# Spectral filter and gated feed-forward, forward and backward: all row-tile transposes in the head, the transform of x as pieces of the loop

## The chip, the core and the metric

The kernel runs on one core of a Trainium2 chip. The metric is the device time of one execution in microseconds (us). TensorE is called PE, its weight loads PEld, VectorE DVE, ScalarE ACT, GpSimd POOL, and SyncE, which issues most DMAs, SP.

## What is computed

The reference is the forward result of a gated mix and the gradients of its inputs:

```python
g = sigmoid((x * gate_w).sum(-1, keepdims=True))       # one gate per row
a = irfft2(rfft2(x) * (w_r + 1j * w_i))                # spectral filter over both axes
b = (gelu(x @ w_gate) * (x @ w_up)) @ w_down           # feed-forward
out = g * a + (1 - g) * b                              # then the gradients by vjp with grad_out
```

x and grad_out (dO below) are 2048 x 576, w_gate and w_up 576 x 4608, w_down 4608 x 576, the filter 2048 x 289, all bf16. Outputs are `out`, the gradients of x, w_r, w_i, w_gate, w_up, w_down, gate_w. The two-dimensional transforms are matrix products with tables of sines: along the 576 columns with `Dt`, along the 2048 rows in two stages, first with `Rt` (within what one row tile holds), and, after a pass through DRAM, with the 32-point table `B`. The same is done for x and for dO, then the products with the filter, then the way back (`RT`, `BT` and `Dt` again).

## The kernel before

**Data.** The rows are dealt out as 16 row tiles of 128. `xn` and `dB` hold x and dO with rows on partitions; `xT` and `dOT` hold them turned, with the 576 columns on partitions in five chunks (the last has 64). A turn of four row tiles (`tchunk`, L335) is 16 full transposes and 8 half ones on PE into three PSUM tiles and three copies to SBUF, of 1024, 1024 and 512 elements per partition.

**Three stages.** The *head* loads x and dO, builds the tables on DVE, ACT and POOL (`build_D`, `build_R`, `columns_B`, `build_B`), turns the row tiles, does the whole forward transform of x, and at its end computes the gate (`gate`, L355, 80 matmuls of one column and a sigmoid). The *loop* goes over 18 groups g of 256 feed-forward columns and, in each, over m = 0 to 3, four row tiles at a time: 72 rounds, called passes here, numbered 4 g + m. The *last part* multiplies what the loop put into DRAM (`scr`) by the weights once more, and forms `out` and the gradients of x and gate_w.

**A pass.** `H_mm` (L370) multiplies dOT by w_down into the PSUM tile z (L380, L383), and xT by w_gate and w_up into two PSUM tiles xy (L387, L394). ACT copies z to `da` (L404), and xy to `q` (squared), `xb` and `hu` (L411 to L414). `H_ew1` (three DVE operations, L419 to L421) gives the argument s of the sigmoid; `H_ew2` is two sigmoids on ACT, om and s (L435, L436), and eight DVE operations (L440 to L447) that leave A, dHg and dHu. SP stores them to `scr`. The tiles q and s have one buffer each. From group 1 on a pass also does a part of the weight gradients of the group before, `W_units`: halves of 16 or 8 matmuls (L480, L497, L510) into a PSUM pool of two buffers, with a copy on ACT (L458) and a DMA from POOL at the end of a unit. `scale_dB` (L932) scales dB by 1 - g in two halves after passes 3 and 4.

**Spectral pieces.** The rest of the transforms is cut into pieces, the list `fft`, which `fft_next` calls one after the other. A forward row tile has two: u1 (L546), six matmuls (L551) and a copy Y on ACT (L556, L558), and u2 (L561), two matmuls (L568), a copy ve on ACT (L572), two DVE operations that leave Vt (L574, L575) and a store to `scr_x` or `scr_g` (L576). `zipped` lists them as u1(0), u1(1), u2(0), u1(2), u2(1) and so on. Behind the 32 pieces of dO come the tables turned for the way back (three pieces), 74 slots of the middle (`mid_units`: s2 with two copies of 64 partitions each, L666, s1 with one copy, L753, and seven empty slots ahead; the products with the filter are DVE work, called in portions by `side_work`), and 64 pieces of the inverse. 175 slots in all. In group 0 pieces take turns in two PSUM tiles, pg and z; from group 1 on the feed-forward's z tile is the only one.

**Order.** It is written by hand: each engine's queue has the instructions in the order in which the program calls them, and an engine waits at its first instruction that isn't ready. `want(pr)` says how many pieces are to be done after a pass: 4 per pass in group 0, and then as many as make an even load up to pass 64, where a slot of the middle counts 1.7. That is 3 or 4 per pass in passes 4 to 10, mostly 2 up to pass 47, and 3 or 4 to pass 64. In a pass of group 1 and later the first piece stands inside the second half of xy, and the next ones between the weight halves, when the weights' nominal time `at` reaches 0, 1, 3 and 5; the sigmoids (`sigs`, which calls `H_ew2`) are put in at 1.0:

```python
for w, f in carry + hs:
    if k < n and at >= (0.0, 1.0, 3.0, 5.0)[k]:
        fft_next()
        k += 1
    if late and at >= 1.0:
        late.pop()()
    f()
    at += w
```

In the head, x's pieces use the same four PSUM tiles as the transposes in turn (`headps`, L330), x's first pieces follow the first four row tiles, and the other turns stand between them. gate_w comes as a column by three small DMAs from POOL (L852, L853).

Of the kernel before, what the change touches and what calls it, by code (L numbers as in the profile page):

```python
# [140 lines left out]
def build_R(nc, tb, unit, t0):  # L141

    V = nc.vector
    n = 4
    step = 2.0 * math.pi / S * EPS_SCALE
    X = unit([n, P], I32, name="XR")
    krow, kadd = tb.kk[:, 0, :], tb.kk[:, 1, :]
    for t in range(n):
        V.scalar_tensor_tensor(X[:, t, :], krow, tb.scol[:, t0 + t:t0 + t + 1], kadd, op0=ALU.mult, op1=ALU.add)
    V.tensor_single_scalar(X[:], X[:], S - 1, op=ALU.bitwise_and)  # L150
    if t0 % 8 == 0:
        tb.Rpair = unit([8, P], name="Rt")
    o = tb.Rpair[:, t0 % 8:t0 % 8 + n, :]
    tb.late.append(lambda: nc.scalar.activation(o, X[:], ACT.Sin, bias=tb.pi[:], scale=-step))
    tb.Rt += [tb.Rpair[:, t0 % 8 + t, :] for t in range(n)]
# [36 lines left out]
def build_B(nc, tb, unit, res):  # L192
# [10 lines left out]
    for s in range(2):  # L203
        G.iota(mask[:, 0, :, :, :, s], pattern=[[0, 2], [1 - 2 * s, 2], [0, 16]], base=s, channel_multiplier=0, **kw)
    X = unit([2, 2, 16, 2], F32, name="XB")
    Xi = unit([2, 2, 2, 16, 2], I32, name="XBi")
# [13 lines left out]
    def sines():  # L220
        nc.scalar.activation(o[:], Xi[:].rearrange("p v a b c d -> p v (a b c d)"), ACT.Sin, bias=tb.pi[:], scale=-step)
        V.tensor_tensor(tb.B[:], o[:], ms[:].rearrange("p v a b c d -> p v (a b c d)"), op=ALU.mult)
    tb.late.append(sines)


@with_exitstack
def kernel(
# [31 lines left out]
    xn = res.tile([P, T, D], BF16, name="xn")  # L259
    gwT = res.tile([P, 5], BF16, name="gwT")  # L260
    xT = hres.tile([P, 5, T, P], BF16, name="xT")
    dOT = hres.tile([P, 5, T, P], BF16, name="dOT")
# [5 lines left out]
    def load_w(g, part):  # L268

        fsl = slice(g * FG, (g + 1) * FG)  # L270
        if part == 0:
            wts[g] = (wpool.tile([P, 5, 2 * FG], BF16, tag="wgu", name="wgu"), wpool.tile([P, 5, FG], BF16, tag="wdT", name="wdT"))
            wgu = wts[g][0]
# [16 lines left out]

    nc.gpsimd.memset(gwT[LO, 4:5], 0.0)
    ident = res.tile([P, P], BF16, name="ident")
# [7 lines left out]

    for k in range(4):
        load_x(4 * k)
    for k in range(4):
        load_do(4 * k)
    load_w(0, 0)

    ew = wstack.enter_context(tc.tile_pool(name="ew", bufs=2))
# [26 lines left out]

    def tchunk(src, dst, t0, copy=None):  # L335
        for k, cs in enumerate(((0, 1), (2, 3), (4,))):
            pool, tag = headps()
            tp_ = pool.tile([P, 2, 2, 4, P], BF16, tag=tag, name="tp")
            for j, c in enumerate(cs):
                for tt in range(4):  # L340
                    if c < 4:
                        nc.tensor.transpose(tp_[:, 0, j, tt, :], src[:, t0 + tt, eo(c)], ident[:])
                    else:
                        for r in (LO, HI):
                            nc.tensor.transpose(tp_[r, 0, 0, tt, :], src[:, t0 + tt, 512:D], ident[:])
            o = dst[:, cs[0]:cs[0] + len(cs), t0:t0 + 4, :]
            i = tp_[:, 0, 0:len(cs)]
            if copy:
                copy(o, i)
            elif k == (t0 // 4) % 2:  # L350
                nc.scalar.copy(o, i)
            else:
                V.tensor_copy(o, i)

    def gate():  # L355
        lps = head_tile()[:, 0]
        for t in range(T):
            for ci in range(5):
                nc.tensor.matmul(lps[:, t:t + 1], lhsT=xT[:, ci, t, :], rhs=gwT[:, ci:ci + 1],
                                 start=(ci == 0), stop=(ci == 4))  # L360
        nc.scalar.activation(g_bf[:], lps[:, 0:T], ACT.Sigmoid)
        V.tensor_copy(g32[:], g_bf[:])
        V.tensor_scalar(omg_bf[:], g32[:], -1.0, 1.0, op0=ALU.mult, op1=ALU.add)
        V.tensor_copy(omg32[:], omg_bf[:])
        V.tensor_scalar(gs32[:], g32[:], SD2, None, op0=ALU.mult)
# [176 lines left out]

    def fwd_units(src, dst, scale, ps=pftile, vevac=None):
        ys = {}
# [16 lines left out]
        def u2(t):  # L561
            def f():
                Y = ys.pop(t)
                R = tb.Rt[t]
                vps = ps()
                Yf = Y[:].rearrange("p e c l -> p (e c) l")
                for o, ys_ in enumerate((Yf[:, 0:4:3, :], Yf[:, 2:0:-1, :])):
                    nc.tensor.matmul(vps[:, o, :2 * HF].rearrange("p (e l) -> p e l", e=2), lhsT=R, rhs=ys_, start=True, stop=True)  # L568
                Vt = (unit if src is xT else half)([2, DF], name="Vt")
                ve = unit([2, 2, HF], F32, name="ve")  # L570
                n0 = 1 if src is xT or on_pg() else 0
                nc.scalar.copy(ve[:, n0:2].rearrange("p o c l -> p o (c l)"), vps[:, n0:2, :2 * HF])  # L572
                v = [vps[:, 0, :2 * HF].rearrange("p (c l) -> p c l", c=2) if n0 else ve[:, 0], ve[:, 1]]
                V.tensor_tensor(Vt[:, :, 0:HF], v[0], v[1], op=ALU.add)  # L574
                V.tensor_tensor(Vt[:, :, DF - 1:HF - 1:-1], v[0][:, :, 0:HF - 1], v[1][:, :, 0:HF - 1], op=ALU.subtract)  # L575
                LD.dma_start(dst[:, t], Vt[:])  # L576
# [263 lines left out]

    def head_tile():
        pool, tag = headps()
        return pool.tile([P, 2, 512], F32, tag=tag, name="fx")

    build_D(nc, tb, unit, res, 0, 2)
    build_D(nc, tb, unit, res, 2, 2)
    tchunk(xn, xT, 0, V.tensor_copy)
    build_D(nc, tb, unit, res, 4, 1)
    columns_B(nc, tb, res)
    with nc.allow_non_contiguous_dma(reason="tiny gate_w column load"):  # L850
        for par in range(2):
            nc.gpsimd.dma_start(gwT[:, 2 * par:2 * par + 2], gate_w[par:512:2].rearrange("(k p) -> p k", p=P))  # L852
        nc.gpsimd.dma_start(gwT[HI, 4:5], gate_w[512:D].rearrange("(p o) -> p o", o=1))  # L853
    x1, x2 = fwd_units(xT, scr_x, None, ps=head_tile)
    build_R(nc, tb, unit, 0)
    run_late(tb)
    for t in range(T):
        x1[t]()
        if t in (6, 11):
            load_w(0, 1 + t // 11)  # L860
        if t % 4 == 2 and t < 14:
            tchunk(xn, xT, t + 2)
        if t >= 9 and t % 2 == 1:
            tchunk(dB, dOT, 2 * (t - 9))
        if t % 4 == 1 and t + 3 < T:
            build_R(nc, tb, unit, t + 3)
        if t == 13:
            build_B(nc, tb, unit, res)
        if tb.late:
            tb.late.pop(0)()  # L870
        if t > 1:
            x2[t - 2]()
    run_late(tb)
    x2[T - 2]()
    x2[T - 1]()
    gate()

    fg = zipped(*fwd_units(dOT, scr_g, gs32))
    ia, pa = inv_units(scr_p1, a_dv, SD2)
# [15 lines left out]
    n_slots = sum(1 for u in fft if not getattr(u, "noslot", False))  # L895
    mid_at = 2 * T + 10
    NPR = NT // 2
    LASTP = NG * NPR - 7
    done = [0]

    def want(pr):

        n0 = 4 * NPR
        if pr < NPR:
            return 4 * (pr + 1)

        def load(n):

            return n + 0.7 * min(max(n - mid_at, 0), n_mid)
        share = load(n0) + (load(n_slots) - load(n0)) * (pr + 1 - NPR) / (LASTP - NPR)  # L910
# [24 lines left out]
    for g in range(NG):  # L935
# [3 lines left out]
        for m in range(NPR):  # L939
# [5 lines left out]
            def side_work(us):  # L945
                while side and us > 0:
                    us -= side[0][0]
                    side.pop(0)[1]()
            if g == 0 and m > 0:
                fft_next()  # L950
            z, xy_full = H_mm(g, m)
# [4 lines left out]
            flush()  # L956
            if g == 0:
                fft_next()
            if pr == 0:
                fft_next()  # L960
            H_act(0, xy, tiles, 1)
            state = []

            def second():
                xy = xy_full(1, fft_next if n or g == 0 else None)
                for part in range(2):
                    H_act(1, xy, tiles, part)
                state.append(H_ew1(tiles))
                side_work(1.4)

            def sigs():
                H_ew2(g, m, tiles, state[0], da)
                side_work(1.4)
            if g == 0:
                second()
                fft_next()
                sigs()
            else:
                second()
                at, k, late = 0.0, min(n, 1), [sigs]  # L980
                for w, f in carry + hs:
                    if k < n and at >= (0.0, 1.0, 3.0, 5.0)[k]:
                        fft_next()
                        k += 1
                    if late and at >= 1.0:
                        late.pop()()
# [5 lines left out]
                if late:  # L992
                    sigs()
            carry = []
            flush(len(stores) - 1)
# [251 lines left out]
```

## Time and profile before

| what | us |
| --- | --- |
| median of five runs | 1455.92 |
| the five runs | 1461.59, 1462.19, 1455.92, 1454.86, 1455.90 |
| the profiled execution's own time | 1461.59 |
| its span, first to last instruction | 1459.8 |
| PE busy in the span | 1395.4 (96%) |
| DVE busy | 731.6 (50%) |
| ACT busy | 715.3 (49%) |
| POOL busy | 125.7 (9%) |
| mean granted PE clock | 0.992 |

The profile is of one execution. Its span leaves 1.8 us of its own time outside. It gives for every instruction the engine, the source line, the tiles that it writes and reads, its start and duration, and for idle time what ended it. A row of a stretch gives, after its limits and length, the busy time of PE, PEld, DVE, ACT and POOL in it with the number of instructions, then the granted clock, the share of the DMA engines and GB/s. A row of waits gives the waiting instruction, what it waited for, the sum, the count and the longest. A row in order of time gives start, duration, engine, line, operation, tiles, and in square brackets the idle time before it. A PE row's duration takes in the drain of its last matmul, so the time from start to start is the shorter and is what a dense stream pays.

### The profile page before, as it was taken

Reading aid. Unit: us, or ns where it says so; the run is one execution under the profiler, and the core shown is the slowest. Engines: PE = TensorE matmul, PEld = TensorE weight load, DVE = VectorE, ACT = ScalarE, POOL = GpSimd, SP = SyncE. Lnnn points to the kernel's source line nnn. Section 1 sums busy time; section 2 is a strip of 40 time slices with the busy share of each in tenths; the row PEclk is TensorE's granted clock in tenths of the full one; section 3 lists DMA queues with packets and bytes.
Section 4 is the critical chain, followed back from the end, with each engine's and each line's share of the span. In section 5 each row is a group of like instructions: output and inputs, shape, how many; then the busy total and the mean of one; then the engine's idle time right before and its main releaser. Section 6 shows DMA issues by size and latency. Waiting matters only on the chain.

```text
span 1459.8 us, 28184 instructions
## 1 busy us (share of the span) xinstructions
PE 1395.4 (96%) x11414; PEld 1024.3 (70%) x11414; DVE 731.6 (50%) x1394; ACT 715.3 (49%) x1311; POOL 125.7 (9%) x230
## 2 busy tenths in 40 slices
PE   6888899998999999999999999999999999999997
PEld 4555675675676667667767767668777777777776
DVE  6676556876776676755656556552000652212200
ACT  5776767777677777666766766663000000000000
POOL 3000010010011011001001001100000110000000
PEclk9999999999999999999999999999999999999999
DMA  5333354544644554463554653848999997887773
GB/s 190 94 103 104 100 162 110 146 120 137 164 121 132 143 157 116 114 170 89 154 145 120 161 156 105 193 126 203 214 192 195 217 205 160 168 160 158 163 148 75
DMA packets 516477, 214.96 MB, mean 147 GB/s; under 512 B 312921, under 2 KB 510554, under 8 KB 516346
## 3 DMA queue, kind: packets, MB, share of 16 engines
q1 hardware_dynamic: 506714, 192.65, 56.4%
q0 software_dynamic: 7824, 19.49, 4.5%
q8 instruction: 89, 1.46, 0.4%
q10 hardware_dynamic: 1808, 1.02, 0.2%
q14 instruction: 42, 0.34, 0.1%
HBM read 40.76 MB, written 93.84 MB: 92 GB/s over the span
## 4 chain that ended last, share of the span: by engine, by line
PE 80%; ACT 9%; DVE 4%; DMA 2%; issue 2%; SPq 1%; POOL 0%; ACTq 0%; DVEq 0%; POOLq 0%
PE acc L1092 29%; PE xy L394 15%; PE wps L497 14%; PE z L380 8%; PE wps L480 6%; PE xy L387 2%; PE wps L510 2%; ACT om L435 2%; PE z L383 1%; ACT xb L413 1%; ACT hu L414 1%; ACT q L411 1%; DMA wd_all<-in_B_w_down_dram 1%; ACT Xx L666 1%; DMA out_dram<-dw 1%
## 5 line engine op out<-in xcount | busy, mean ns | idle before, releaser
L1092 PEld LDWEIGHTS <-pin 128*128 128x128 bf16 x3456 | 338.3, 98 | 87.6 <-issue 1.5
L394 PE MATMUL xy<-wgu,xT 128*128 128x512 bf16 x1152 | 272.6, 381 | 0.0
L497 PEld LDWEIGHTS <-xn 128*128 128x128 bf16 x2304 | 224.6, 98 | 38.0 <-issue 0.2
L394 PEld LDWEIGHTS <-xT 128*128 128x128 bf16 x1152 | 106.4, 98 | 137.1 <-issue 30.9
L404 ACT ACTIVATE da<-z,omg 128x256 bf16<-128x256 f32 x288 | 112.8, 474 | 117.8 <-PE z L383 117.8
L480 PE MATMUL wps<-dB,A 128*128 128x288 bf16 x1152 | 152.1, 286 | 12.4 <-ACT dwd L458 12.4
L1109 ACT COPY bo<-acc 128x288 f32<-128x288 f32 x32 | 12.8, 399 | 308.2 <-PE acc L1092 250.1
L380 PE MATMUL z<-wdT,dOT 128*128 128x256 bf16 x1152 | 139.0, 274 | 14.8 <-ACT Y L558 4.2
L1092 PE MATMUL acc<-wgT,pin 128*128 128x288 bf16 x1152 | 145.3, 288 | 0.8 <-ACT dw L458 0.8
L480 PEld LDWEIGHTS <-A 128*128 128x128 bf16 x1152 | 112.1, 98 | 45.7 <-issue 15.0
L1092 PE MATMUL acc<-wuT,pin 128*128 128x288 bf16 x1152 | 143.6, 286 | 0.0
L1092 PE MATMUL acc<-wd_all,pin 128*128 128x288 bf16 x1152 | 142.6, 286 | 0.0
L380 PEld LDWEIGHTS <-dOT 128*128 128x128 bf16 x1152 | 112.2, 98 | 34.6 <-issue 19.9
L497 PE MATMUL wps<-dHg,xn 128*128 128x256 bf16 x1152 | 135.8, 273 | 0.0
L497 PE MATMUL wps<-dHu,xn 128*128 128x256 bf16 x1152 | 133.8, 273 | 0.0
L411 ACT ACTIVATE q<-xy 128x512 bf16<-128x512 f32 x144 | 86.9, 604 | 55.9 <-PE xy L394 54.0
L419 DVE TENSOR_SCALAR s<-q 128x1024 bf16<-128x1024 bf16 x72 | 30.7, 426 | 159.5 <-ACT q L411 159.5
L440 DVE TENSOR_TENSOR xb<-xb,s 128x1024 bf16<-128x1024 bf16 x72 | 49.9, 693 | 108.3 <-ACT s L436 108.3
L503 POOL DMA_DIRECT2D out_dram<-dw x67 | 48.8, 728 | 632.0 <-ACT dw L458 526.9
L1169 DVE SCALAR_TENSOR_TENSOR f32t<-gwf,dlog,b16t 128x576 f32<-128x576 f32 x16 | 13.1, 817 | 173.7 <-DMA b16t<-dxa_scr 173.7
L414 ACT CAST hu<-xy 128x512 bf16<-128x512 f32 x144 | 88.3, 613 | 0.0
L413 ACT CAST xb<-xy 128x512 bf16<-128x512 f32 x144 | 84.8, 589 | 0.0
(197 smaller groups left out, 1594.3 us busy)
## 6 DMA issues: line engine op xcount, KB each, us to landing
scr<-A SPq DMA_DIRECT2D x72, 256.0 KB, 2.6
scr<-dHg SPq DMA_DIRECT2D x72, 256.0 KB, 2.8
scr<-dHu SPq DMA_DIRECT2D x72, 256.0 KB, 3.3
out_dram<-dw POOLq DMA_DIRECT2D x67, 128.0 KB, 2.3
wd_all<-in_B_w_down_dram SPq DMA_DIRECT2D x3, 1728.0 KB, 16.6
out_dram<-dwd POOLq DMA_DIRECT2D x34, 144.0 KB, 2.9
scr_p<-Vt SPq DMA_DIRECT2D x32, 145.0 KB, 3.5
wgu<-in_B_w_gate_dram SPq DMA_DIRECT2D x18, 256.0 KB, 3.7
```

Of the source, the lines that this page charges most:

```text
L380: nc.tensor.matmul(zo(t), lhsT=dOT[:, ci, t, :], rhs=wdT[:, ci, :], start=(t % 4 < 2 and ci == 0), stop=False)
L394: nc.tensor.matmul(xy[k][:, t % 2, :], lhsT=xT[:, ci, t, :], rhs=wgu[:, ci, :], start=False, stop=(ci == 3))
L404: nc.scalar.activation(da[:, t, :], z[:, t % 2, t // 2, :], ACT.Copy, scale=omg32[:, 4 * m + t:4 * m + t + 1])
L411: nc.scalar.activation(q[:, h, :], xy[:, :, 0:FG], ACT.Square)
L413: nc.scalar.copy(xb[:, h, :], xy[:, :, 0:FG])
L414: nc.scalar.copy(hu[:, h, :], xy[:, :, FG:2 * FG])
L419: V.tensor_scalar(s[:], q[:], A_GELU, 1.0, op0=ALU.mult, op1=ALU.add)
L440: V.tensor_tensor(xb[:], xb[:], s[:], op=ALU.mult)
L480: nc.tensor.matmul(wps[:, :288], lhsT=tl(0, t)[:, fch * P:(fch + 1) * P], rhs=dB[:, t, h * 288:(h + 1) * 288], start=(t == 0), stop=(t == ...
L497: nc.tensor.matmul(wps[:, cc, :], lhsT=xn[:, t, (c0 + cc) * P:(c0 + cc + 1) * P], rhs=tl(k, t), start=(t == 0), stop=(t == T - 1))
L503: wst[0].dma_start(ov[:, c0:c0 + TPB, fsl], dw[:])
L1092: nc.tensor.matmul(acc[:, :288], lhsT=src[:, r, :], rhs=w_of(r)[:, h * 288:(h + 1) * 288], start=(first and r == 0), stop=(last and r == F ...
```

## The change

It does six things.

1. The head turns all row tiles of x and dO, in the order x, dO, x, dO, and does nothing of the transform of x. Which engine copies each of the three PSUM tiles of a turn is written out by hand (`VC` is a DVE copy, `AC` an ACT copy).
2. The transform of x becomes the first 32 pieces of `fft`, which now has 207 slots. x's Vt takes the pool `half` of two buffers, as dO's did.
3. Group 0 does 0, 1, 1 and 2 pieces in its four passes (`FIRST` holds the sums). Later passes share the rest evenly up to pass 64, with a slot of the middle counting 1.5: 3 in pass 4, 4 each in passes 5 to 18, 2 or 3 (4 in passes 20 and 21) up to pass 49, and 4 each in passes 50 to 64.
4. In a pass with four or more pieces they stand at 0, 1, 2, 3.6 and 5, and the sigmoids at 1.6. `side_work` takes larger portions.
5. R tables 8 to 15 and the table B are begun in group 0, between passes; their sines on ACT run at the end of pass 4.
6. SP loads x and dO in turns, with the transposing loads of w_down's first group after the first of each. gate_w comes as a row by one DMA from SP, and five matmuls with a 1 x 1 tile of one turn it into the column.

```diff
+    gwr = unit([D], name="gwr")
+    LD.dma_start(gwr[0:1, :], gate_w.rearrange("(o d) -> o d", o=1))
+    load_x(0)
+    load_do(0)
+    load_w(0, 1)
+    for k in range(1, 4):
         load_x(4 * k)
-    for k in range(4):
         load_do(4 * k)
     load_w(0, 0)
+    load_w(0, 2)
...
-                Vt = (unit if src is xT else half)([2, DF], name="Vt")
+                Vt = half([2, DF], name="Vt")
...
+    gps = head_tile()[:, 0]
+    for c in range(5):
+        w = gwr[0:1, eo(c)] if c < 4 else gwr[0:1, 512:D]
+        r = slice(0, P) if c < 4 else HI
+        nc.tensor.matmul(gps[r, c:c + 1], lhsT=w, rhs=one[:], start=True, stop=True)
+    AC(gwT[:, 0:4], gps[:, 0:4])
+    AC(gwT[HI, 4:5], gps[HI, 4:5])
     build_D(nc, tb, unit, res, 0, 2)
+    turn(xn, xT, 0, (VC, VC, AC))
     build_D(nc, tb, unit, res, 2, 2)
-    tchunk(xn, xT, 0, V.tensor_copy)
+    turn(dB, dOT, 0, (AC, VC, AC))
     build_D(nc, tb, unit, res, 4, 1)
+    turn(xn, xT, 1, (VC, VC, AC))
+    turn(dB, dOT, 1, (AC, VC, VC))
+    build_R(nc, tb, unit, 0)
+    build_R(nc, tb, unit, 4)
+    turn(xn, xT, 2, (VC, AC, VC))
+    run_late(tb)
+    turn(dB, dOT, 2, (AC, VC, VC))
+    turn(xn, xT, 3, (AC, VC, VC))
+    gate(head_tile)
+    turn(dB, dOT, 3, (AC, VC, AC))
     columns_B(nc, tb, res)
-    x1, x2 = fwd_units(xT, scr_x, None, ps=head_tile)
-    build_R(nc, tb, unit, 0)
-    run_late(tb)
-    for t in range(T):
-        x1[t]()
...
-            x2[t - 2]()
...
-    fg = zipped(*fwd_units(dOT, scr_g, gs32))
+    makeB = build_B(nc, tb, unit, res)
+    fg = zipped(*fwd_units(xT, scr_x, None)) + zipped(*fwd_units(dOT, scr_g, gs32))
...
-    mid_at = 2 * T + 10
+    mid_at = 4 * T + 10
+    FIRST = (0, 1, 2, 4)
...
-            return n + 0.7 * min(max(n - mid_at, 0), n_mid)
+            return n + 0.5 * min(max(n - mid_at, 0), n_mid)
...
-                side_work(1.4)
+                side_work(1.9)
             def sigs():
                 H_ew2(g, m, tiles, state[0], da)
-                side_work(1.4)
+                side_work(2.4)
             if g == 0:
                 second()
-                fft_next()
+                for _ in range(n - 1):
+                    fft_next()
                 sigs()
+                if m == 0:
+                    next(makeB)
+                elif m < 3:
+                    build_R(nc, tb, unit, 4 * m + 4)
+                else:
+                    next(makeB)
             else:
                 second()
                 at, k, late = 0.0, min(n, 1), [sigs]
+                spots, sig_at = ((0.0, 1.0, 3.0), 1.0) if n < 4 else ((0.0, 1.0, 2.0, 3.6, 5.0, 5.0), 1.6)
                 for w, f in carry + hs:
-                    if k < n and at >= (0.0, 1.0, 3.0, 5.0)[k]:
+                    if k < n and at >= spots[k]:
                         fft_next()
                         k += 1
-                    if late and at >= 1.0:
+                    if late and at >= sig_at:
                         late.pop()()
...
+                if pr == NPR:
+                    run_late(tb)
```

`turn` is the three items of the old `tchunk` with the copy named for each. `build_B` is now a generator of two steps: the first sets up the POOL patterns, the second does the DVE part and leaves the sine for `run_late`.

## The prediction

> **What bounds the kernel now.** I read the stretches first: busy time per engine, cut at the first matmul of z (L380) in passes 0, 4, 6 and 10, then at the ends of the spectral work. A pass is one round of the loop over (g, m), 72 in all; a piece is one call of fft_next.
>
> ```profile
> core 0: us, PE busy (x) PEld busy (x) DVE busy (x) ACT busy (x) POOL busy (x), PEclk, DMA share, GB/s
> 0.00:50.03 50.03, 35.05 (x400) 25.53 (x401) 35.55 (x109) 29.57 (x53) 12.92 (x46) 0.97 0.47 161
> 50.03:96.40 46.37, 36.79 (x236) 20.62 (x233) 27.70 (x55) 33.55 (x64) 0.00 (x0) 0.93 0.37 106
> 96.40:126.68 30.28, 28.46 (x232) 20.08 (x232) 24.29 (x51) 20.85 (x37) 2.39 (x4) 1.00 0.39 110
> 126.68:184.26 57.58, 51.19 (x384) 34.90 (x382) 28.87 (x54) 38.56 (x72) 3.88 (x6) 0.97 0.35 100
> 184.26:640.00 455.74, 441.10 (x3523) 310.28 (x3521) 316.43 (x580) 330.05 (x597) 45.23 (x71) 1.00 0.50 137
> 640.00:925.00 285.00, 279.17 (x2361) 201.00 (x2360) 169.08 (x298) 199.00 (x366) 26.57 (x42) 1.00 0.50 134
> ```
>
> TensorE (PE) is without work for 15.0 us in the head, 9.6 in group 0 (passes 0 to 3), then 1.8, 6.4, 14.6 and 5.8. So the program is PE's from pass 5 on, and only head and group 0 are another engine's. Whatever shortens these by moving PE work into the loop gets most of it billed there. Next, the order of time in group 0:
>
> ```profile
> 73.47 1.06 ACT L436 ACTIVATE s<-s 128x1024 bf16<-128x1024 bf16 x1
> ...
> 74.56 0.69 DVE L440 TENSOR_TENSOR xb<-xb,s 128x1024 bf16<-128x1024 bf16 x1 [2.08 <-ACT s L436]
> 75.28 0.69 DVE L441 TENSOR_TENSOR q<-xb,q 128x1024 bf16<-128x1024 bf16 x1
> 76.01 0.69 DVE L442 TENSOR_TENSOR om<-om,q 128x1024 bf16<-128x1024 bf16 x1
> ...
> 79.14 0.69 DVE L447 TENSOR_TENSOR dHg<-hu,om 128x1024 bf16<-128x1024 bf16 x1
> 79.75 0.45 DVE L574 TENSOR_TENSOR Vt<-pf,ve 128x290 bf16<-128x290 f32 x1
> ```
>
> A pass of group 0 is a ring through ACT and DVE: two sigmoids, eight DVE operations, and then a piece's Vt, for which PE's next piece waits. Its period is 12 us (om starts at 60.16 and 72.38). Last, what PE waits for in the loop, 112 to 170 us and then 170 to 430:
>
> ```profile
> PE z L380 <- ACT ve L572: 1.9, 1, 1.9
> PE pf L551 <- ACT ve L572: 1.9, 1, 1.9
> PE z L380 <- ACT Y L558: 0.8, 1, 0.8
> ```
> ```profile
> PE wps L480 <- ACT dwd L458: 6.1, 5, 1.7
> ```
>
> From group 1 on all pieces share PSUM tile z with the feed-forward: when a piece's copy stands behind the two sigmoids on ACT, the next z or piece waits up to 1.9 us.
>
> **1. Head.** It keeps 64 + 64 row transposes with their copies, the D tables, R tables 0 to 7 and the gate. It loses x's 32 pieces (on DVE 16 x (0.458 + 0.447), on ACT 16 x (0.642 + 0.404)), R 8 to 15 and the B tables. DVE: 35.55 - 14.5 - 3.1 - 2.9 - 1.0 (copies moved to ACT) = 14.1 us. ACT: 29.57 - 18.7 (pieces, two R sines, oB) + 1.6 = 12.5. They serve the same tiles in turns, so the head lies between 19 (DVE alone, from its first full work at 5) and 31 us (one behind the other). I walked the two queues in the new order with the rows' durations (copies 0.68 and 0.42 on DVE, 1.02 and 0.57 on ACT, an R table 1.52): last x copy 21.8, gate 2.1, last dO transposes 1.4, their last copy, which frees PSUM tile z, 26.3. Loads: SP now issues the w_down transposes ahead of row tiles 4 to 15; at the 314 and 229 GB/s of the first 20 us the 5.6 MB of the head are in by 20, and the five copies into wdT (0.66 each to issue, 2.2 to land) by 24. That is hidden behind the copies, by 2 us only. Three gate-column issues leave POOL, one 1.1 KB load joins SP.
>
> PE's clock: the first 16 transposes took 1.89 us, later ones 1.05; after the 2.3 us wait at 22, six matmuls took 1.66 instead of 0.91; one z took 3.27 instead of 1.91. In the new head PE does little but transposes. Between nothing and 4.6 us (gate 2.1, transposes 1.1, z 1.4) lie on the path; I take 1.5. First z at **27.8** instead of 50.05.
>
> The Trainium skill (TensorE: Matmul & The Clock Gate, Part 4: PE-mode transpose) says that transposes don't count as activity for the gate, and Part 1 of that page that the array starts at half rate. The trace doesn't settle it: transposes at full rate stood beside other matmuls there. By that rule the whole 4.6 us would be paid.
>
> **2. Group 0.** It now has 0, 1, 1, 2 pieces instead of 4 each. om(0) comes 8.0 us after z (q 4.5, two sets of three copies, s on DVE). After om: sigmoids 2.1, L440 to L442 2.1 (tile q has one buffer, so the next q waits for them), q, xb, hu 1.5, Y 0.65, q 0.55, s 1.2, and some DVE queueing: 8.6. An R table behind the eight operations makes it 10.05; with Vt 10.8; before pass 4 the B table (1.9), scaling dB (2.3) and Vt make it 13.7. om(4) at 35.8 + 43.15 = 78.95 against 107.83. PE needs 6 to 7 us of each of these, so it is covered even at half rate. Late sines: pass 4 gets a table load, two R sines and oB (3.2 us) on ACT, ahead of da(5), and a second load before om(5). z(5) waits for a copy ahead of them; da(5) is 0.4 late. Pass 5 (15.9 of PE, one piece more) hides the rest; without cover it costs 4.5. Its z, and pass 6, come at 82.2 and **98.1 instead of 126.68: -28.6**.
>
> The skill (ScalarE: Activation LUTs, What ACT_TABLE_LOAD costs) prices a switch at about 2.66 us: 1.28 for the load and the rest for a drain behind it. The trace's row of the load agrees, and after the one at 48.68 ACT waits for PE only, so the drain isn't seen there. Two added switches would be an estimated 5.3 us by the page, against 2.6 by the row.
>
> **3. Pieces owed.** By pass 6 before had done 32 + 22, after 11: 43 remain. In the dense stream the six matmuls of a u1 take 0.75 and the two of a u2 0.25 (starts 116.24, 116.99; 118.83, 119.08): 21 pairs and one = **+21.8**. On ACT they are 1.2 a pair, on DVE 0.8, on SP one store; passes of 14 us at four pieces need 9.6 of ACT: beside PE. x's Vt now has two buffers instead of the large pool; a store lands in 2.0 us, and two come per pass.
>
> **4. Waits in passes 6 to 19**, now four pieces each. Walk of m = 0: PE ends piece 2 at 8.8 after z, the third at 11.3, and after one dwd half is at piece 4 at 12.3; ACT ends ve 9.55, sigmoids 11.6, dw 12.1, Y 12.75: wait 0.55. m = 2 has 0.65, m = 1 and 3 none: 1.3 a group, three groups; passes 6 and 7, with one weight unit, 2.2 each: 8.3. Before, passes 6 to 9 took 57.58 for 49.6 of matmuls: z and xy 6.05 a pass, halves of weight units at 1.74 and 0.98 (42.5 together), 7.1 of pieces. So 8.0. **+0.3**.
>
> **5. Middle.** The 74 slots now run in passes 20 to 48, 2 or 3 a pass, instead of 10 to 45, mostly 2. A third piece in m = 0 or 2 has its copies (s2 two of 0.64, s1 0.84) behind sigmoids and dw: z waits 0.4 to 1.7, mean 1.1, eight times = 8.8. The dwd wait of m = 1 (1.25) comes in 7 groups instead of 9. That is 17.6, against 15.0 that PE waits there now (9 x 1.25, and 3.7 in single waits for copies, which I take to be of the kind counted): **+2.6**. DVE has 7.0 per pass and 11.2 per product set: 32.2 of 39 us in three passes, against 39.2 of 51 in four: still under. Inverse pieces at 4 instead of 3.5: about 4.5 of waits against 5: **-0.5**. What follows the loop doesn't change.
>
> **Sum**: -28.6 + 21.8 + 0.3 + 2.6 - 0.5 = -4.4; span 1455.4, time 1457.2 against the profiled 1461.59, which itself is 5.7 above the median 1455.92. On the median: 1451.5, said as **1451**, own range 1445 to 1457.
>
> **Rivals.** B, the crowded passes don't wait: sigmoids start earlier than I walked, third pieces in the middle find ACT free. For it: with two pieces, z nearly never waits there. Against: the 1.9 us rows. 1451.5 - 8.8 = 1443. C, slower: every third piece in the middle waits the full 1.9 us of those rows, in all 17 passes that have one: 32.3 instead of 8.8, so 1474; it passes +0.5% from 11 such passes on (+12 us). For it: ACT is 72% busy there already and one PSUM tile turns everything over. Against: s1 copies are 0.84, and in m = 3 3.5 us of matmuls cover. D, the change doesn't do what it says: DVE and ACT alternate in the head until 31, and group 0 keeps its 12 us ring: 1451 + 3 + 5 = 1459.
>
> **Chances.** A measurement of this kernel can't tell less than 0.5% (7.3 us; 1448.6 and 1463.2) from no change. A (forecast) 0.46, of which 0.13 lies below 1448.6; B 0.33; C 0.13; D 0.08, of which 0.01 slower. Faster 0.46, same 0.40, slower 0.14. The range 1439 to 1466 takes in A, the unknown 3 us of the clock, most of B and the near half of C; some 0.18 is out.
>
> **What would show it.** First z near 28 and pass 6 near 98; PE idle of some 10 us in the head and 15 in passes 0 to 4; in passes 6 to 19 waits of pf for Y of about 0.6; in 20 to 48 z waiting for Vt or Xg. Wrong if pass 6 comes after 104, if PE idle from pass 6 to the end of the pieces is under 15 us (B) or over 45 (C).

## The result, and the profile after

| | us |
| --- | --- |
| before, median of 65 runs (1453.98 to 1462.19) | 1457.97 |
| changed, median of 37 runs (1450.53 to 1459.35) | 1455.64 |
| ratio, 95% interval | 0.9983 [0.9977, 0.9988] |
| forecast | 1451, range 1439 to 1466 |
| changed, the profiled execution's own time and span | 1457.6 and 1455.8 |

The change gains 0.17% where I forecast about 0.3%. By the bound of the prediction that is no change; I had given "faster" the larger chance. From `H_mm` on, the line numbers of the changed kernel are six higher (L386 for L380). In the profiles the first z of these passes starts at:

| | before | forecast | changed |
| --- | --- | --- | --- |
| pass 0 | 50.05 | 27.8 | 26.22 |
| pass 4 | 96.40 | | 64.03 |
| pass 5 | 111.04 | 82.2 | 83.23 |
| pass 6 | 126.68 | 98.1 | 101.26 |
| pass 20 | 314.74 | | 300.99 |
| pass 71 | 982.54 | 978.1 | 981.20 |

(The 978.1 is the sum of the prediction, -4.4, put on the 982.54.) So 25.4 us are won by pass 6, and 24.1 of them are given back by pass 71. The stretches of the changed kernel show where. The cuts are the first z of passes 0, 4, 6, 20, 49 and 65:

```profile
core 0: us, PE busy (x) PEld busy (x) DVE busy (x) ACT busy (x) POOL busy (x), PEclk, DMA share, GB/s
0.00:26.20 26.20, 17.89 (x277) 15.34 (x278) 17.00 (x56) 14.93 (x24) 5.72 (x22) 0.91 0.78 256
26.20:64.03 37.83, 30.11 (x180) 16.34 (x180) 22.68 (x47) 26.44 (x50) 4.25 (x20) 0.91 0.24 66
64.03:101.26 37.23, 32.93 (x235) 21.88 (x234) 26.97 (x65) 25.66 (x43) 2.60 (x4) 0.88 0.34 100
101.26:300.99 199.73, 193.40 (x1527) 135.53 (x1525) 115.07 (x212) 141.88 (x256) 17.12 (x27) 1.00 0.39 114
300.99:680.66 379.67, 367.98 (x2925) 258.13 (x2922) 273.39 (x509) 285.81 (x513) 36.40 (x58) 1.00 0.54 142
680.66:908.40 227.74, 219.56 (x1878) 158.22 (x1878) 135.62 (x239) 160.23 (x290) 21.08 (x33) 1.00 0.50 136
```

Length less PE's busy time is PE's idle time: 8.3 in the head, 7.7 in group 0, 4.3 in passes 4 and 5, then 6.3, 11.7 and 8.2. Before, the head and group 0 had 15.0 and 9.6. From pass 6 to the end of the pieces it is 26.2, as before (6.4 + 14.6 + 5.8 = 26.8): the loop stayed PE's, and the pieces that moved into it were billed. The granted clock is 0.91, 0.91 and 0.88 up to pass 6 and 1.00 behind it. In order of time, the first half of z (L386) in passes 0, 4, 5 and 6, with the waits:

```profile
26.22 3.57 PE L386 MATMUL z<-wdT,dOT 128*128 128x256 bf16 x16 [0.68 <-ACT dOT L357]
...
64.03 3.57 PE L386 MATMUL z<-wdT,dOT 128*128 128x256 bf16 x16 [3.79 <-ACT Y L562]
...
83.23 3.38 PE L386 MATMUL z<-wdT,dOT 128*128 128x256 bf16 x16 [3.95 <-ACT ve L578]
...
101.26 1.91 PE L386 MATMUL z<-wdT,dOT 128*128 128x256 bf16 x16
```

The same 16 matmuls take 1.91 in a dense stream, and 3.4 to 3.6 in passes 0, 4 and 5, at half rate. The granted clock shows it too. Cut where it changes:

```profile
18.02:21.43 3.41, 3.14 (x32) 2.76 (x31) 1.57 (x4) 1.83 (x3) 0.00 (x0) 0.50 0.38 101
21.43:24.85 3.42, 3.42 (x107) 3.15 (x104) 1.50 (x6) 2.20 (x4) 0.00 (x0) 1.00 0.62 171
24.85:31.68 6.83, 6.15 (x37) 3.39 (x35) 1.84 (x11) 2.62 (x6) 3.83 (x18) 0.50 0.06 14
62.40:69.22 6.82, 5.19 (x25) 2.80 (x25) 4.77 (x13) 4.23 (x8) 0.00 (x0) 0.50 0.36 104
82.88:86.29 3.41, 3.06 (x15) 2.13 (x15) 3.34 (x7) 3.38 (x6) 2.04 (x3) 0.50 0.23 63
```

In pass 4 the half rate is covered: om there waits for s on DVE, and comes as long after om of pass 0 as forecast. In passes 0 and 5 it isn't.

One difference of the two profiles is hardly the change's. What follows pass 71 takes 477.3 us in before's and 474.6 in after's, and between 472.4 and 478.3 in the other runs, none of which edits it. In before's profile 3.4 us of it, from 1035 on, are at a granted clock of 0.50; no other profile has such a stretch between pass 71 and its last 10 us. So the two spans differ by 4.0 and the medians by 2.3.

### The profile page after: what moved, and what is told of

The parts are those of the page before. It is cut to its first block, busy times and chain, and to the rows that moved or that the text cites. A ratio compares the mean times of both kernels' runs of the same rounds, so it can differ in the third digit from the quotient of the medians.

```text
span 1455.8 us, 28140 instructions
## 1 busy us (share of the span) xinstructions
PE 1398.9 (96%) x11419; PEld 1026.4 (71%) x11419; DVE 731.1 (50%) x1393; ACT 727.3 (50%) x1318; POOL 122.9 (8%) x226
## 4 chain that ended last, share of the span: by engine, by line
PE 76%; ACT 12%; DVE 4%; issue 3%; DMA 3%; SPq 2%; POOL 0%; ACTq 0%; DVEq 0%; POOLq 0%
PE acc L1101 29%; PE xy L400 14%; PE wps L503 10%; PE z L386 8%; PE wps L486 6%; ACT om L441 3%; PE xy L393 2%; PE z L389 1%; ACT dw L464 1%; PE pf L557 1%; PE wps L516 1%; ACT ZT L805 1%; ACT s L442 1%; ACT xb L419 1%; ACT q L417 1%
## 5 line engine op out<-in xcount | busy, mean ns | idle before, releaser
L386 PE MATMUL z<-wdT,dOT 128*128 128x256 bf16 x1152 | 142.4, 279 | 18.5 <-ACT ve L578 5.4
L386 PEld LDWEIGHTS <-dOT 128*128 128x128 bf16 x1152 | 113.7, 100 | 40.0 <-issue 23.5
```

Of the source, the lines that this page charges most:

```text
L386: nc.tensor.matmul(zo(t), lhsT=dOT[:, ci, t, :], rhs=wdT[:, ci, :], start=(t % 4 < 2 and ci == 0), stop=False)
```

## The experiments

Theory at the start: the mechanism is the prediction's (pieces go from a stretch that ACT and DVE bound into one that PE bounds, and are paid there), and the lost 3 us are half-rate matmuls in passes 0 and 5. Rivals: the tables that run late, the few pieces in group 0, or new waits in crowded passes took the gain.

### What the pieces of x cost in each place

In the kernel before:

```diff
-            st[p, "vx"] = load_V(scr_x, p)
+            st[p, "vx"] = load_V(scr_g, p)
...
-        x1[t]()
...
-        if t > 1:
-            x2[t - 2]()
```

> Leaves out x's 32 spectral pieces in the head of the kernel before (the middle reads dO's transform in place of x's, so the outputs that depend on x's spectrum are not the reference's). Theory (the pieces cost the head what DVE and ACT take for them, since the head is a ladder of these two): DVE 35.6 - 14.5 = 21 us, ACT 29.6 - 16.8 = 13, first z of pass 0 at 25 to 29 instead of 50.05, time 21 to 25 us less than before. Rival (the head waits for loads and transposes anyway): less than 12 us less.

Measured 1438.87 against 1458.30 for before beside it, ratio 0.9863 [0.9848, 0.9877]: 19.4 us, just under the theory's band and far from the rival's (first z at 30.58, also outside what was expected). The same in the changed kernel:

```diff
-    fg = zipped(*fwd_units(xT, scr_x, None)) + zipped(*fwd_units(dOT, scr_g, gs32))
+    fg = [gap] * (2 * T) + zipped(*fwd_units(dOT, scr_g, gs32))
```

> Leaves out the same 32 pieces where the changed kernel has them; their slots stay, empty, so the rest keeps its passes (the middle reads dO's transform in place of x's). Theory (the loop bills them at TensorE's price, 0.5 us a piece, and a few waits): 16 us of matmuls, some 5 of waits in passes 6 to 11, 1 to 3 in group 0: 19 to 24 us less than the changed kernel, and so nearly what they cost in the head before. Rival (the pieces cost the loop more than their matmuls, by queueing on ACT): over 30 us less. Rival (they are free, covered by waits): under 8 us less.

Measured 1432.06: 23.6 less than the changed kernel. It is 6.2 ahead at pass 5, 8.8 at pass 6, 24.9 at pass 12 and 24.7 at pass 71. So the pieces are paid where they run, 16.1 us for 21 of them in passes 6 to 11. By these two prices moving them is a loss of some 4 us (23.6 in the loop, 19.4 in the head, each known to 2 or 3 us), and the rest of the change makes up for it.

### The sigmoids behind the pieces' copies

In the changed kernel ACT's queue in pass 6 has this order (dw is the copy of a unit of the weight gradients):

```profile
110.26 0.64 ACT L578 COPY ve<-pf 128x580 f32<-128x580 f32 x1 [0.43 <-PE pf L574]
110.80 1.06 ACT L441 ACTIVATE om<-s 128x1024 bf16<-128x1024 bf16 x1
111.89 1.06 ACT L442 ACTIVATE s<-s 128x1024 bf16<-128x1024 bf16 x1
112.86 0.57 ACT L464 CAST dw<-wps 128x512 bf16<-128x512 f32 x1
113.32 0.65 ACT L562 CAST Y<-pf 128x580 bf16<-128x580 f32 x1
```

and PE's row for the matmuls that need that Y is:

```profile
114.02 0.41 PE L574 MATMUL pf<-Y,Rt 128*128 128x290 bf16 x2 [1.30 <-ACT Y L562]
```

The copy Y could follow its matmuls, which started at 111.81 and took 0.91; it stands behind two sigmoids and dw. The edit puts the sigmoids later in the list:

```diff
-  spots, sig_at = ((0.0, 1.0, 3.0), 1.0) if n < 4 else ((0.0, 1.0, 2.0, 3.6, 5.0, 5.0), 1.6)
+  spots, sig_at = ((0.0, 1.0, 3.0), 3.0) if n < 4 else ((0.0, 1.0, 2.0, 3.6, 5.0, 5.0), 4.0)
```

> The changed kernel with the sigmoids put later among the weight halves: at 3.0 in passes of up to three pieces and at 4.0 in the others, so that ACT copies the pieces and weight units ahead of them. Theory (what TensorE still waits for in the loop are copies that stand behind the two sigmoids on ACT): most of 6 + 12 + 8 us of such waits go, 12 to 22 us less than the changed kernel. Rival (ACT is simply full, the wait only moves): within 3 us of the changed kernel, the waits under other names.

Measured 1433.46, ratio 0.9822 [0.9804, 0.9839]: 22 us less, the upper end. Its stretches, cut at the same passes (6, 20, 49, 65):

```profile
98.77:294.46 195.69, 192.77 (x1526) 135.34 (x1524) 114.76 (x208) 144.03 (x258) 17.17 (x27) 1.00 0.42 116
294.46:668.04 373.58, 368.23 (x2924) 258.94 (x2922) 275.54 (x511) 286.98 (x513) 37.36 (x58) 1.00 0.54 145
668.04:887.41 219.37, 218.44 (x1881) 158.28 (x1879) 135.70 (x239) 160.05 (x290) 20.43 (x32) 1.00 0.52 142
```

They are 4.0, 6.1 and 8.4 shorter, and PE's idle time in them is 2.9, 5.4 and 0.9 instead of 6.3, 11.7 and 8.2. Another 2.5 are won ahead of pass 6. Nothing was taken out of the work. Of the 5.4, one wait is new: matmuls of the middle waited 3.6 for a load of pair 1.

Is it the sigmoids alone, or only together with the change? The sigmoids at 3.0 in the kernel before:

```diff
-                    if late and at >= 1.0:
+                    if late and at >= 3.0:
```

> The kernel before with the sigmoids at 3.0 instead of 1.0 in its passes. Theory (the same copies stand behind the sigmoids there, 6 + 15 + 6 us in the loop): 10 to 18 us less than before, 1440 to 1448, so that the change is worth 7 to 14 us once these waits are gone from both. Rival (the change is worth nothing in any loop): within 3 us of the changed kernel with late sigmoids, 1433.

Measured 1451.84, 0.9946 [0.9928, 0.9965]: 6.0 less, so both numbers missed. What PE waited for there from 640 to 1000 us (ev, ZU and ZT are copies of the inverse's pieces):

```profile
PE z L380 <- ACT ev L828: 4.5, 4, 1.6
PE xy L394 <- issue: 3.7, 23, 0.2
PE z L380 <- ACT ZU L811: 2.4, 2, 1.2
PE z L380 <- ACT ZT L799: 1.5, 1, 1.5
```

With before's places a fourth piece comes at 5.0, directly ahead of the next pass's z, which waits for its copy. So late sigmoids should pay only where the pieces' places leave room. With the places of the change and late sigmoids, x still in the head:

```diff
+  spots, sig_at = ((0.0, 1.0, 3.0), 3.0) if n < 4 else ((0.0, 1.0, 2.0, 3.6, 5.0, 5.0), 4.0)
-                    if k < n and at >= (0.0, 1.0, 3.0, 5.0)[k]:
+                    if k < n and at >= spots[k]:
```

> The kernel before with the changed kernel's places for four pieces (0, 1, 2, 3.6) and with late sigmoids (3.0 and 4.0), so that only the move of x's transform and what goes with it tells it from the changed kernel with late sigmoids. Theory (28.6 forecast and 25.4 found before pass 6, less x's price of 19.9 without the waits): 5 to 10 us more than that kernel's 1433.5, so 1439 to 1443, and the rest of the 18 us by which late sigmoids alone helped less in the kernel before was its places at 5.0. Rival (the move of x itself is worth some 18 us once the sigmoids are late): 1450 to 1453.

Measured 1440.91, 0.9874 [0.9851, 0.9896], 11 us less than with before's places. (In passes of four pieces the sigmoids went from 3.0 to 4.0 as well; the two weren't run apart.) And the changed kernel with before's places and its sigmoids at 1.0:

```diff
-  spots, sig_at = ((0.0, 1.0, 3.0), 1.0) if n < 4 else ((0.0, 1.0, 2.0, 3.6, 5.0, 5.0), 1.6)
+  spots, sig_at = (0.0, 1.0, 3.0, 5.0), 1.0
```

> The changed kernel with the places of the kernel before: pieces at 0, 1, 3 and 5, sigmoids at 1.0, whatever the number of pieces. Theory (by the walk of a pass, the new places are worth about 0.2 us in two passes of four, 30 passes have four pieces): 0 to 5 us more than the changed kernel. Rival (the new places are what lets four pieces into a pass): 12 us more or worse.

Measured 1458.71, 1.0001 [0.9990, 1.0012]. That makes a table of ratios to before:

| | x in the head | x in the loop |
| --- | --- | --- |
| before's places, sigmoids at 1.0 | 1 | 1.0001 |
| the change's places and sigmoids | | 0.9983 |
| the change's places, late sigmoids | 0.9874 | 0.9822 |

The move of x with all that goes with it is worth nothing with the old places and 0.5% (7.5 us) with late sigmoids. The change's 0.17% is as large as what its new places and sigmoids bring, 0.18%. The pieces without waits:

> The changed kernel with late sigmoids and without x's 32 pieces (slots empty, the middle reads dO's transform in place of x's). Theory (16 of the 23.6 us that the pieces cost in the changed kernel are matmuls, the rest waits behind the sigmoids): 16 to 19 us less than 1433.5. Rival (the price is ACT's and DVE's): 22 to 25 less again.

(The edit that empties x's slots and that of the late sigmoids, together.) Measured 1413.58: 19.9 less than with the pieces, a little above the band. So of the 23.6 that x costs in the changed kernel some 4 are waits and 20 are the pieces, 0.62 each.

### The late tables, and the start of the loop

R tables 8 to 15 and B whole in the head again:

```diff
-    makeB = build_B(nc, tb, unit, res)
+    for _ in build_B(nc, tb, unit, res):
+        pass
+    build_R(nc, tb, unit, 8)
+    build_R(nc, tb, unit, 12)
+    run_late(tb)
...
-                if m == 0:
-                    next(makeB)
-                elif m < 3:
-                    build_R(nc, tb, unit, 4 * m + 4)
-                else:
-                    next(makeB)
```

> The changed kernel with R tables 8 to 15 and table B made whole in the head, so that group 0 and pass 4 are free of them and of two table loads. Theory (the forecast's price for passes 0 to 5 was short by 4.7 us because the ladder of group 0 and the cold clock were dearer, not the late tables): head 4 to 6 us longer, passes 0 to 5 some 5 shorter, time within 2.5 us of the changed kernel. Rival (the late tables are the missing 4.7 us): 3 to 6 us less.

Measured 1456.31, 0.9982 [0.9971, 0.9993], the same as the changed kernel; first z at 26.81, pass 5 at 85.35 and pass 6 at 101.39. The om of pass 0 comes at 43.93 instead of 36.93, since the tables now stand ahead of it on ACT and DVE; 4.9 of these 7.0 are saved up to om of pass 4, and the other 2 in pass 5, whose z took 1.91 here, after a wait of 1.41. So moving the tables back doesn't bring the lost 3 us. Then the clock, with matmuls whose result nobody reads, eight in each pass of group 0:

```diff
+  idle = pg.tile([P, 2, 512], F32, tag="pg", name="idle")
+  for k in range(8):
+      nc.tensor.matmul(idle[:, k % 2, :], lhsT=ident[:],
+                       rhs=xT[:, k % 4, 0:4, :].rearrange("p t m -> p (t m)"), start=True, stop=True)
```

> The changed kernel with eight further matmuls of 512 columns in each pass of group 0, into a PSUM tile that nobody reads. Theory (part of the 4.7 us by which passes 0 to 5 were longer than forecast is TensorE's half clock after idle time): z of passes 4 and 5 take 1.9 us instead of 3.6 and 3.4, pass 6 begins 2 to 4 us earlier, the time falls by as much. Rival (the ladder on ACT and DVE alone sets it): no change, or up to 3 us more.

Its z of passes 4 and 5:

```profile
67.57 3.14 PE L386 MATMUL z<-wdT,dOT 128*128 128x256 bf16 x16
...
81.99 1.91 PE L386 MATMUL z<-wdT,dOT 128*128 128x256 bf16 x16 [0.35 <-ACT ve L578]
```

Pass 5's z is at full rate, pass 6 comes at 98.54 instead of 101.26 and pass 71 at 978.27 instead of 981.20. Not all of the 2.7 at pass 6 is due to the idle matmuls. The om of pass 0 in the changed kernel, and then here with the first idle matmuls:

```profile
36.93 1.06 ACT L441 ACTIVATE om<-s 128x1024 bf16<-128x1024 bf16 x1 [0.33 <-DVE s L426]
```
```profile
33.58 1.89 PE L979 MATMUL idle<-xT,ident 128*128 128x512 bf16 x8
35.68 1.06 ACT L441 ACTIVATE om<-s 128x1024 bf16<-128x1024 bf16 x1 [0.34 <-DVE s L426]
```

1.2 us are there already at this om, which needs nothing that stands behind the idle matmuls: the half rate over z of pass 0 ended at 29.12 in this execution, and at 31.68 in the other. From om of pass 0 to om of pass 4 it is 43.1 in both. The 1.5 that are left come in pass 5. There the idle matmuls did it by taking away the pause: they put z of pass 4 3.5 us later, so that z of pass 5 waited 0.35 instead of 3.95. By the medians the gain is 1.4 (1454.27, 0.9972 [0.9960, 0.9984]); this interval and that of the changed kernel overlap. So in these two profiles more work on PE makes pass 5 shorter; that it makes the kernel shorter isn't shown. Then useful work in the same place, with more pieces in group 0:

```diff
-    FIRST = (0, 1, 2, 4)
+    FIRST = (2, 4, 7, 10)
```

> The changed kernel with 2, 2, 3, 3 pieces in group 0 instead of 0, 1, 1, 2. Theory (group 0 is a ladder of ACT and DVE, so a piece costs it about 0.7 us there, against 0.5 of matmuls and some wait saved later): within 2.5 us of the changed kernel. Rival (TensorE's idle time in group 0 takes the pieces free): 3 to 6 us less.

Measured 1460.06, 1.0015 [1.0004, 1.0026]: 4.4 more than the changed kernel, which neither side expected. Pass 6 comes only 1.1 later, pass 71 4.9. The loss is in passes 20 to 48, which take 8.0 more (3.0 come back behind them): all later pieces now fall on other passes. z waits 5.4 us for the copy Vt there, against 0.8 in the changed kernel; the rest isn't traced.

### A faster version, and how it breaks

Late sigmoids, busy group 0, and the loads of pair 1 issued beside those of pair 0:

```diff
-                    if p == 0:
-                        prefetch(p + 1)
...
             prefetch(0)
+            prefetch(1)
```

> Changed kernel with late sigmoids, with the eight idle matmuls per pass of group 0, and with the second load of the middle put beside the first (the one wait of 3.6 us that late sigmoids brought in, for Vp from scr_x). Theory (these two waits add up with the rest): 3 to 7 us less than 1433.5. Rival (TensorE-bound, the gains don't add): within 1.5 us of it.

Measured 1427.30, 0.9787 [0.9765, 0.9809], the fastest of all: 28 us under the changed kernel, 31 under before, and 6.2 under late sigmoids alone, in the theory's band. The idle matmuls and the load weren't run apart. Passes 20 to 48:

```profile
292.85:660.35 367.50, 361.87 (x2896) 258.10 (x2923) 275.42 (x511) 286.86 (x513) 37.21 (x58) 1.00 0.54 147
```

They are 6.1 shorter than with late sigmoids alone, more than the 3.6 of the wait. The same with no pieces in group 0, four slots later (`FIRST = (0, 0, 0, 0)`):

> The kernel late_busy_pre with no pieces in group 0 at all. Theory (a piece costs the ladder of group 0 0.8 us and the loop 0.5 to 0.6 once the waits are gone): 0.5 to 2 us less than late_busy_pre. Rival (idle time of TensorE there takes pieces free): 2 us more.

Measured 1491.70, 1.0228 [1.0203, 1.0253]: 64 us more, the largest miss of the study. In passes 20 to 48, ACT's copies of the middle's Vt waited 61.1 us for Vt's own stores (six times, up to 13.4), and behind them PE's z 51.3. One such Vt, SP's queue ahead of its store, and what followed:

```profile
423.09 0.85 ACT L757 CAST Vt<-pf 128x580 bf16<-128x580 f32 x1
...
428.95 0.81 SPq L632 DMA_DIRECT2D Vp<-scr_x  x1
429.81 0.84 SPq L632 DMA_DIRECT2D Vp<-scr_g  x1
430.70 2.93 SPq L658 DMA_DIRECT2D Wt<-in_A_w_r_dram  x6
433.67 2.89 SPq L658 DMA_DIRECT2D Wt<-in_A_w_i_dram  x6
436.66 3.81 SPq L759 DMA_DIRECT2D scr_p<-Vt  x3
...
439.28 0.81 ACT L757 CAST Vt<-pf 128x580 bf16<-128x580 f32 x1 [12.93 <-DMA scr_p<-Vt]
...
440.14 3.57 PE L386 MATMUL z<-wdT,dOT 128*128 128x256 bf16 x16 [10.17 <-ACT Vt L757]
```

This Vt was ready at 423.9, and that in the other of the two buffers at 426.1. Their stores stand behind weight loads (up to 427.2), three stores of the feed-forward and fourteen loads that take 7.7 us to issue. So the third copy Vt, and with it ACT, waits until the first store has landed, and PE waits for ACT. z then runs at half rate. To test that order, the loads go behind the pair's last store:

```diff
-                if key == "m1" and b == 1 and p + 2 < T // 2:
-                    prefetch(p + 2)
...
                 LD.dma_start(dst[g:g + 2].rearrange("g q l -> q g l"), Vt[:])
+                if key == "n1" and b == 1 and p + 2 < T // 2:
+                    prefetch(p + 2)
```

> The version without pieces in group 0 again (1491.7), with the two loads and twelve table loads of pair p + 2 issued behind the last of pair p's four stores instead of ahead of the second. Theory, the waits of up to 10.7 us for Vt in the middle are SP's order: the stores that free Vt's two buffers stand behind 14 load issues and what these wait for. Then ACT's 61 us of waits for the store and PE's 51 us go, and with them the half-rate z behind each: 1425 to 1440. Rival, the pieces themselves fall in the wrong places of the pass (a third piece next to the other two), whatever SP does: not under 1475.

Measured 1460.22, 0.9996 [0.9982, 1.0009]: 31 of the 64 us go, between the two bands. ACT's wait for Vt's stores falls from 61.1 to 25.7 and PE's for Vt from 51.3 to 13.8, with 5.6 new for wdT. So the order ahead of the stores is about half of it. What the other half is stays open. The same move in the fastest version:

> The same move of the loads in the fastest version (1427.3, one piece in each of passes 1 and 2 and two in pass 3). Theory: ACT waits 5.2 us for stores of Vt there and PE next to nothing, so 0 to 2 less. Rival, the loads come too late behind the stores and PE waits for X or W: 3 or more slower.

Measured 1470.78, 1.0079 [1.0061, 1.0097]: 3% slower than without the move, the theory wrong by far. Of what PE waited for between 300 and 720 us the first row is

```profile
PE pf L667 <- DMA Vp<-scr_x: 29.5, 6, 7.0
```

Here the loads come too late. One queue has to carry both. With the loads ahead it was fast at one place of the pieces and slow at the other (1427.3 and 1491.7), with the stores ahead slow at both (1470.8 and 1460.2).

## Why the prediction was wrong, point by point

| step | forecast | measured |
| --- | --- | --- |
| in-order walk of the head, without the clock | 26.3 | 26.2 |
| first z to om of pass 0 | 8.0 | 10.7 |
| om of pass 0 to om of pass 4 | 43.15 | 43.1 |
| pass 5 | 15.9 | 18.0 |
| PE idle, passes 6 to 19 | 8.3 | 6.3 |
| PE idle, passes 20 to 48 | 17.6 | 11.7 |
| PE idle, passes 49 to 64 | 4.5 | 8.2 |
| given back from pass 6 to 71 | 24.2 | 24.1 |

**The mechanism was right.** Head and group 0 gave what they had, and it was billed in the loop almost to the us. The two in-order walks (ACT and DVE in the head, the ring of group 0) came out within 0.1.

**The step that failed is "PE's clock": "I take 1.5", between bounds of nothing and 4.6.** I saw the danger for the gate, the transposes and the first z. The transposes at half rate cost next to nothing, the copies covered all but the last eight (0.64 instead of 0.41). From first z to om of pass 0 it took 2.7 more, of which 2.3 stand in PE's rows: from z to the long part of xy it is 4.90 there, and 2.60 in pass 1. That is no single bad execution: in nine other profiles of kernels that begin like this one, om comes 9.5 to 10.9 after z instead of the 8.0 forecast. And I called all that follows "covered even at half rate", then let pass 5, which is PE's, run its z at full rate. Its z stood behind a wait of 3.95 us that my own walk of group 0 contained, and ran at half rate: 1.5. Together 4.2 instead of 1.5; with 0.6 more in pass 5 that no run puts down to the clock (it took 16.55 with a full-rate z, in the run with idle matmuls), pass 6 is at 101.3 instead of 98.1. That run took the 1.5 back. PE was idle 11.7 us in passes 0 to 4 where I had named 15: matmuls at half rate fill idle time without doing more.

**The base.** The sum of -4.4 stands beside -4.0 between the spans, but that closeness is luck: 2.7 of the 4.0 is the last part of the one execution I measured against, and at pass 71 it was 1.3. And the five runs' median lay 2.0 under that of 65. True gain 2.3 instead of 4.4, from a base 2.0 higher: 1455.6 instead of 1451.

**Right in sum, not in its terms.** The 24.2 of the loop against 24.1 is luck in part. The 8.0 that I took for the kernel before in passes 6 to 9 had in it 1.4 of a half-rate z (pass 7, 3.27); the changed kernel has none there. Waits in the middle were fewer than walked and those behind pass 49 more; 43 pieces at the dense price of 0.51 look too cheap, where x's alone measured 0.62 without waits. With PE as idle as before from pass 6 on, nearly all of the 24.1 is pieces.

**The rivals.** B (waits vanish) had 0.33 and is refuted for this kernel: 26.2 us of idle PE from pass 6 to 64, not under 15. It was a rival about the wrong thing: with other places of the sigmoids the waits do vanish, and that is 22 us. C's waits of 1.9 in every third piece didn't come (longest 1.7, in a few passes). D's head of 31 us didn't come either. Most of the chance of "faster" was B's; without B the forecast itself, 0.3%, lay below the 0.5% that I took a measurement to tell.

**Transposes and table loads.** On transposes and the clock (TensorE: Matmul & The Clock Gate, Part 4: PE-mode transpose) the head decides. From 5.20 to 21.9 PE does only transposes; among their rows are

```profile
7.59 1.89 PE L353 MATMUL fx<-ident,dB 128*128 128x128 bf16 x16
...
10.06 1.59 PE L353 MATMUL fx<-ident,xn 128*128 128x128 bf16 x16
...
13.90 1.07 PE L353 MATMUL fx<-ident,xn 128*128 128x128 bf16 x16
...
19.80 1.83 PE L353 MATMUL fx<-ident,xn 128*128 128x128 bf16 x16
```

They reach full rate by themselves after some 6.5 us, and fall back after a wait of 2.4 at 15.9. By the page's rule all would have been slow. Here the measurement stands against it, at least as an absolute rule: the clock fell once more at 24.85, as the rows above show, while PE did the gate and transposes without a pause. On table loads (ScalarE: Activation LUTs, What ACT_TABLE_LOAD costs) the page prices a drain behind each load. The first one added:

```profile
83.47 1.28 ACT L154 ACT_TABLE_LOAD   x1
84.77 1.34 ACT L154 ACTIVATE Rt<-XR,pi 128x512 bf16<-128x512 int32 x2
```

The next operation starts 0.02 behind the load's end, and the second load, at 95.52, is followed as closely. The price was 1.3 each, as the row of before had it.

## What to carry to other kernels

Work moved from a stretch that another engine bounds into one that PE bounds is paid there nearly in full; forecast the difference of two prices (here 19.4 and 23.6), not the gap that it leaves. After each long wait of PE in the new order (here 3.8 and 3.95 us) ask whether the matmuls behind it are on the path, and price them at half rate if they are. And look at what stands in an in-order queue ahead of a copy or store that frees a buffer: two sigmoids put later were worth 22 us, some ten times the whole change, and moving fourteen loads behind the stores was worth 31 us in one version and cost 43 in another.

## What was not expected of the hardware

A z at half rate follows waits of 3.8 and 3.95 us (3.57 and 3.38), and after waits of 0.35 and 0.73 it took 1.91. But that of pass 0 also took 3.57, after only 0.68 of waiting, behind transposes of which the last full ones ran at full rate (1.05 for 16) and the half ones at half (0.64 for 8 instead of 0.41). The granted clock changes in steps: in all 16 profiles its half-rate stretches last 3.41 us, or two or three times that, but for the one at the very end. The one over z of pass 0 had begun at 24.85, ahead of z and behind 6.5 us without a pause (gate and transposes). In profiles of kernels with the same head the stretch that covers this z lasted 3.41 in some, 6.83 or 10.24 in others. How long the matmuls must run, and which pauses and which work count, these runs don't settle. With eight idle matmuls in a pass one z was at full rate and another still at 3.14.
